# First batch's remainder moved to the third batch, zero tile first, and late halves ahead of the last block's values

## The chip, the cores and the metric

The kernel runs on one core of one Trainium2 chip. The metric is the time on the device in microseconds (us). A core has five engines with their own queues: PE (matmul), DVE (vector), ACT (scalar), POOL (GpSimd) and SP, which here only issues transfers. PE writes to PSUM; DVE and ACT read PSUM; POOL works on SBUF only and also issues transfers.

## The reference, cut to what matters

Batch is 8, heads 8, sequence 576, head size 64; the feed-forward part has 4608 rows of 512 and a hidden size of 1536.

```python
kv = einsum('bhsd,bhse->bhde', k, v)          # per head 64 x 64, no softmax
o  = einsum('bhsd,bhde->bhse', q, kv)
x  = o / sqrt(mean(o*o, -1) + 1e-6) * g_norm  # norm over the head
x  = x.transpose(0, 2, 1, 3).reshape(4608, 512)
xn = x / sqrt(mean(x*x, -1) + 1e-6) * rms_g   # norm over the row
out = (silu(xn @ w_gate) * (xn @ w_val)) @ w_out
```

## The kernel before, in words

**Tiling.** A batch has 576 rows: four chunks of 128 (512 "main" rows) and a remainder of 64. The feed-forward part runs in nine groups of 512 rows: the main rows of each of the eight batches, and one group (number 8, run as the last but one) of the eight remainders, whose x is gathered in the tile `xr`. A group has 24 slots, a gate and a value product for each of 12 blocks of 128 hidden columns (`slots_a`, four matmuls of 512 columns each), and 16 slots of the output product (`slots_b`). Gate goes through silu on ACT (L686), value is multiplied with it on DVE (L695, tile `h`).

**Attention.** For a batch the kernel computes k times v (`kv`), q transposed (`qT`), o, the two sums of squares that both norms need, and from them one factor per row and head (`chain`), then `xna` = o times factor, and x as the transpose of it. In batches 2 to 7 this is placed among the slots of the group before: `place_attention` hands every operation to a planner (`Placer`), which knows a cost and a room per slot and engine and puts an operation in the first slot in which it fits; `P.at` books one at a fixed slot. There the squares are made on ACT (L391, tile `sq`), weighted on POOL (L446), summed on DVE (L454), the product `xna` on DVE (L521, L526), and the transposes are transfers issued by SP (L336 and L338 for q, L583 for x). Batch 1 is placed by hand among the slots of group 0 (`place_second`, its base slot as argument). Inside one slot the operations are issued in the order of booking, PE's behind the slot's own matmuls. All engines take their instructions in that order.

**The lead.** Batch 0 comes first and by hand. PE spins on a tile of zeros, `idle` (`spin`, L238), until k times v can start (`kv_pairs`, L291); chunks 0 and 1 are taken up to x, and then group 0 begins with the first half of its rows (256 columns, L705 and L677) while the weights are still on their way in four blocks (`wg`, `wv`, issued by POOL, L228 and L229). The list `early` holds 22 slots: slot 0 has the first block's three gates, then come its three values, then three gates and three values for each other block. After each slot n, `behind(n)` issues a piece of the attention of chunks 2 and 3 and of the remainder: q's transposes (L310), o transposed (L404), the sums (L429), the chain, o (L371), `xna` (L381) and x's transposes (L552). Then come 12 slots "half" with gate and value of the late 256 rows, and 16 slots "all" of output. POOL casts the remainder of batch 0's q (L216), which SP loads (`load_rem`, L202), and goes on with the loads of batch 1, the output weights (L233) and k and v of batch 2.

**Order of transfers.** A load waits in the queue of the engine that issues it, for what that engine does before it. Some are tied to others by hand: the late half of the first q to the first v, the second broadcast of g to the last gate weights, q of batch 2 to the first output weights.

Of the kernel before, what the change touches and what calls it, by code (L numbers as in the profile page):

```python
# [87 lines left out]
def kernel(  # L88
# [47 lines left out]

    ident = consts.tile([128, 128], BF16, name="ident")
# [22 lines left out]
    for tile_, rows in ((krT, REM // 2), (vr, REM // 2), (rems[0][0], REM)):  # L160
        for r0 in (rows, 2 * rows) if rows < REM else (rows,):
            nc.vector.memset(tile_[r0 : REM if r0 < REM else 128], 0.0)
    idle = consts.tile([128, MAIN], BF16, name="idle")
    nc.vector.memset(idle, 0.0)  # L164
# [78 lines left out]
    class Att:  # L243
        def __init__(self, b):
            self.b = b
            self.kv, self.qT = kvs[b % 2], qTs[b % 2]
            if b < 2:
                self.qTj = self.qT.rearrange("p c j t -> p (c j t)").rearrange("p (j c t) -> p j c t", j=NS, c=NC + 1)
            else:
                self.qTj = self.qT.rearrange("p c j t -> p j c t")  # L250
            self.kv_chunks = range(NC + 1)
            self.o, self.outa, self.sq = {}, {}, {}
            self.xT = {}
            self.st = None
# [79 lines left out]
        def qT_dma(self):  # L334
            flat = mains[self.b, 0].rearrange("p c h d -> p (c h d)")
            nc.sync.dma_start_transpose(out=self.qT[:, 0:NC].rearrange("p c j t -> p (c j) t"), in_=flat)  # L336
            rem = rems[0][self.b % 2][:REM].rearrange("p h d -> p (h d)")
            return nc.sync.dma_start_transpose(out=self.qT[:, NC, :, 0:REM], in_=rem)  # L338

        def o_mm(self, c, pool=None):  # L340
            self.o[c] = o = (pool or att_p).tile([128, H, D], FP32, name={None: "att"}.get(pool, "mm1" if pool is mm1_p else "o2"))
            for j in range(NS):
                nc.tensor.matmul(  # L343
                    o[:, 2 * j : 2 * j + 2, :], lhsT=self.qTj[:, j, c, :], rhs=self.kv[:, j, :, :],
                    start=j == 0, stop=j == NS - 1, skip_group_check=True,
                )
# [14 lines left out]
        def part(self, t, n):  # L361

            if n == NC:
                return t[:, NC]
            return t[:, n // 2 * 2 : n // 2 * 2 + 2, n % 2 : H : 2]
# [11 lines left out]
        def xna_pairs(self, o, js, c0, c1):  # L377
            if not hasattr(self, "xna"):
                self.xna = xna_p.tile([128, NC + 1, H, D], BF16, name="xna")
            h0, h1 = 2 * js[0], 2 * js[-1] + 2  # L380
            nc.vector.tensor_tensor(  # L381
                out=self.xna[:, c0:c1, h0:h1], in0=o,
                in1=self.al[:, c0:c1, h0:h1].to_broadcast([128, c1 - c0, h1 - h0, D]), op=OP.mult,
            )

        def o_of(self, c):
            return self.o[c] if c == NC else self.o["main", c].rearrange("p c h d -> p (c h) d")
# [60 lines left out]
        def red(self, c, which):  # L448
            if self.st is None:
                self.st = stat.tile([128, 2, NC + 1, H], FP32, name="st")  # L450
# [3 lines left out]
            nc.vector.reduce_sum(out=self.part(self.st[:, which], c), in_=of, axis=AX.X)  # L454

        def chain_t(self):
            if not hasattr(self, "al"):
                t = lambda n, dt=FP32, h=H: stat.tile([128, NC + 1, h], dt, name=n)
                self.u, self.r, self.t, self.z, self.nt, self.al = (t(n) for n in ("u", "r", "t", "z", "nt", "al"))
                self.s = stat.tile([128, NC + 1], FP32, name="srow")  # L460
                self.y = t("y", I32)
# [55 lines left out]
        def xna_(self, c, eng, src=None):  # L517
            if not hasattr(self, "xna"):
                self.xna = xna_p.tile([128, NC + 1, H, D], BF16, name="xna")
            if src is None and c < NC:  # L520
                return eng.tensor_tensor(  # L521
                    out=self.part(self.xna, c), in0=self.outa[c].rearrange("p (c h) d -> p c h d", c=2),
                    in1=self.part(self.al, c).to_broadcast([128, 2, H // 2, D]), op=OP.mult,
                )
# [51 lines left out]
        def x_dma(self, c0, c1):  # L576
            if c0 < NC:
                to = self.x_to()[:, c0:c1].rearrange("p c j t -> p (c j) t")
                of = self.xna[:, c0:c1].rearrange("p c h d -> p (c h d)")
            else:  # L580
                to = xr[:, :, self.b * REM : (self.b + 1) * REM]
                of = self.xna[:REM, c0].rearrange("p h d -> p (h d)")
            return nc.sync.dma_start_transpose(out=to, in_=of)  # L583
# [12 lines left out]
    def place_attention(P, b, casts=(), at=0, chain_at=0):  # L596
        a, start = Att(b), at + 2
        V, A = nc.vector, nc.scalar
        N1 = range(NC + 1)
# [7 lines left out]
        for c in N1:  # L607
            p = P.psum(0.24, lambda: a.o_mm(NC), kv + qt) if c == NC else main
            s = P.put("ACT", 0.6, lambda c=c: a.sq_(c), [p])
            outs[c] = P.put("ACT", 0.6, lambda c=c: a.outa_(c), [p])  # L610
            if c >= 2:
                P.tiles[-1 if c == NC else c - 4] += [s, outs[c]]
# [5 lines left out]
        for n in range(0, 13, 4):  # L618
            prev = [P.put("DVE", 0.8, lambda n=n: [f() for f in a.chain(0, NC + 1)[n : n + 4]], prev, chain_at)]
        xn = [P.put("DVE", 0.68, lambda c=c: a.xna_(c, V), prev + [outs[c]]) for c in N1]  # L620
        put = [P.put("SP", 0.0, lambda c=c: a.x_dma(*c), [xn[c[1] - 1]]) for c in ((0, 2), (2, 4), (4, 5))]
# [200 lines left out]
    load_rem(0, 0)  # L822
# [4 lines left out]
    G.memset(rems[0][1][REM:], 0.0)  # L827
# [55 lines left out]
    cast_rem(0, 0, G)  # L883
# [3 lines left out]
    wo_loads = [load_wo(n) for n in range(NF // OB)]  # L887
    for f in loads_kv(2):
        f()
# [8 lines left out]
    steps = {6: (0, 3), 7: (3, 5), 8: (5, 8), 9: (8, 10), 10: (10, 12)}  # L898

    def behind(n):  # L900
# [4 lines left out]
        elif n == 1:  # L905
            a.qT_out(a.qT_mm(ALL, (NC,)), ALL, NC, A)
# [3 lines left out]
        elif n == 4:  # L910
            a.sqT_(a.oT_mm(ALL, NC, NC + 1, o2_p), ALL, NC, NC + 1)
        elif n == 5:
            a.st = None
            a.stat_pairs(P0, 2, 4, att_p, "att")
            a.stat_pairs(P1, 2, 4, att_p, "att")
        elif n == 6:
            a.stat_pairs(ALL, NC, NC + 1, att_p, "att")
        if n in steps:
            for f in a.chain(2, NC + 1)[slice(*steps[n])]:
                f()  # L920
        if n in (8, 9):
            held[n - 8] = a.o_pairs((P0, P1)[n - 8], 2, 4, att_p, "att")
        elif n == 10:
            held[2] = a.o_pairs(ALL, NC, NC + 1, o2_p, "o2")
        if n in (12, 13):
            i = (12, 13).index(n)
# [3 lines left out]
        if n in (15, 16):  # L930
            i = (15, 16).index(n)
# [8 lines left out]
    for n, s in enumerate(early):  # L940
        if n == 12:
            gate = nc.sync.dma_start(out=gbc, in_=g_norm.partition_broadcast(128))
            tc.add_manual_dep(gate.ins, w_loads[-1][0].ins.name, SYNC, reason="the weights come first")
        emit([s])
        behind(n)

    gsq = consts.tile([128, D], FP32, name="gsq")
    G.tensor_tensor(out=gsq, in0=gbc, in1=gbc, op=OP.mult)
    G.tensor_copy(out=g2, in_=gsq.rearrange("p (o d) -> p o d", o=1).to_broadcast([128, H, D]))
    gate = load_q(2)  # L950
    tc.add_manual_dep(gate.ins, wo_loads[0].ins.name, SYNC, reason="the weights come first")
# [11 lines left out]
    for b in range(1, B):  # L963
        if b == 1:
            end = place_second(P, 9)
# [14 lines left out]
        elif b + 1 < B:  # L980
            P.put("SP", 0.0, lambda b=b: load_q(b + 1), at=starts[b - 1] + 6 * (b == 2))
            casts = place_casts(P, b + 1, starts[b - 1] + 18)
            for n, f in enumerate(loads_kv(b + 1)):
                if b == 2:
                    P.at("POOL", 0.85, f, starts[1] + 11 + n)
                else:
                    P.put("POOL", 0.85, f, at=starts[b - 1] + 14)
    emit(slots)
# [28 lines left out]
```

## Time and profile before

| | |
|---|---|
| median of 3 runs | 323.86 us (323.74 to 324.04) |
| profiled execution | 323.98 us |
| its span, first to last instruction | 322.2 us |
| PE busy | 313.7 us |
| DVE busy | 175.4 us |
| ACT busy | 142.9 us |
| POOL busy | 89.0 us |

How to read it: the span leaves out what lies around the instructions, so it is shorter than the time. PE's matmuls overlap and their ends are modelled; for the pace of a run of matmuls the chain of work that ended last is used, which gives pieces with a start, a length and a count. In a timeline the bracket behind an instruction says how long its engine stood idle before it and what ended that. For transfers a row gives the queue, the size and the median time from issue to landing.

### The profile page before, as it was taken

The page shows a single profiled execution, that of the slowest core. Times are in us where ns is not written, and L with a number is a line of the kernel's source. Part 1 is how long each engine was busy: PE and PEld are TensorE (multiplying, and loading weights), DVE is VectorE, ACT ScalarE, POOL GpSimd, SP SyncE. Part 2 cuts the span into 40 slices and gives each one's busy share as a digit, 9 for nine tenths or more (in the row PEclk, how much of TensorE's full clock was granted, in tenths as well). Part 3 has the DMA queues.
Part 4 walks back from the last instruction along what each step waited for, and adds up shares of the span by engine and source line. Part 5 has one row for each costly group of instructions (what it writes and reads, how often), then busy time and mean ns, then how long its engine had stood idle before and what let it go on. Part 6 is the DMA issues. An engine that isn't in the chain of part 4 may idle for free.

```text
span 322.2 us, 5618 instructions
## 1 busy us (share of the span) xinstructions
PE 313.7 (97%) x2158; PEld 160.0 (50%) x2158; DVE 175.4 (54%) x394; ACT 142.9 (44%) x267; POOL 89.0 (28%) x110
## 2 busy tenths in 40 slices
PE   5999999999999999999999999999999999999995
PEld 1678866544444444444444444444444444444443
DVE  4558437487938671768176917781678133203410
ACT  1375466486659322932283227422742233223321
POOL 8763330039006700670058005800420000000000
PEclk9999999999999999999999999999999999999999
DMA  8999999959664994598559956798000600040002
GB/s 213 220 200 199 194 221 220 220 146 144 139 162 130 124 162 141 145 122 144 150 160 102 141 149 181 90 136 167 36 1 0 171 35 0 1 110 22 0 33 100
DMA packets 78358, 40.51 MB, mean 126 GB/s; under 512 B 41976, under 2 KB 73852, under 8 KB 78332
## 3 DMA queue, kind: packets, MB, share of 16 engines
q0 software_dynamic: 30672, 14.16, 34.5%
q1 hardware_dynamic: 46176, 25.01, 31.4%
q10 hardware_dynamic: 1484, 0.99, 1.0%
q8 instruction: 17, 0.28, 0.4%
q14 instruction: 9, 0.07, 0.1%
HBM read 37.78 MB, written 9.44 MB: 147 GB/s over the span
## 4 chain that ended last, share of the span: by engine, by line
PE 97%; DVE 1%; ACT 1%; issue 0%
PE mm L677 58%; PE o L712 27%; PE mm L238 3%; PE att L275 2%; PE mm L712 2%; PE att L343 1%; PE o L356 1%; PE att L552 1%; PE mm L291 0%; PE att L356 0%; PE mm L739 0%; PE o L739 0%; PE mm L705 0%; PE att L321 0%; ACT sqT L415 0%
## 5 line engine op out<-in xcount | busy, mean ns | idle before, releaser
L695 DVE TENSOR_TENSOR h<-silu,mm 128x512 bf16<-128x512 bf16 (+1 forms) x120 | 75.6, 631 | 83.0 <-PE mm L677 73.7
L686 ACT ACTIVATE silu<-mm 128x512 bf16<-128x512 f32 (+1 forms) x120 | 66.4, 557 | 84.2 <-PE mm L677 77.1
L677 PE MATMUL mm<-x,wv 128*128 128x512 bf16 (+1 forms) x432 | 99.9, 356 | 0.0
L677 PE MATMUL mm<-x,wg 128*128 128x512 bf16 (+1 forms) x420 | 98.5, 358 | 0.5 <-DVE h L695 0.5
L712 PE MATMUL o<-wo,h 128*128 128x512 bf16 x396 | 90.1, 379 | 0.0
L446 POOL TENSOR_TENSOR sq<-sq,g 128x512 bf16<-128x512 bf16 x30 | 34.3, 1153 | 130.2 <-ACT sq L391 130.1
L677 PEld LDWEIGHTS <-wv 128*128 128x128 bf16 x480 | 46.2, 98 | 45.2
L677 PEld LDWEIGHTS <-wg 128*128 128x128 bf16 x468 | 45.0, 98 | 45.4 <-issue 1.0
L712 PEld LDWEIGHTS <-h 128*128 128x128 bf16 x420 | 40.2, 98 | 46.0 <-DVE h L695 0.2
L728 ACT COPY osb<-o 128x512 f32<-128x512 f32 x33 | 19.2, 586 | 69.1 <-PE o L712 69.1
L454 DVE TENSOR_REDUCE st<-sq 128x8 f32<-128x512 bf16 x60 | 38.4, 677 | 1.8 <-POOL sq L446 1.7
L304 DVE CAST kvs<-att 64x256 bf16<-64x256 f32 x14 | 5.9, 422 | 30.0 <-PE att L275 29.8
L521 DVE TENSOR_TENSOR xna<-outa,al 128x512 bf16<-128x512 bf16 x24 | 15.0, 684 | 0.0
L238 PE MATMUL mm<-idle 128*128 128x512 bf16 x27 | 8.7, 493 | 4.0 <-DVE idle L164 4.0
L677 PE MATMUL mm<-xr,wg 128*128 128x512 bf16 x48 | 12.3, 379 | 0.0
L677 PE MATMUL mm<-xr,wv 128*128 128x512 bf16 x48 | 12.3, 379 | 0.0
L209 POOL CAST main_q<-stg 128x1024 bf16<-128x1024 f32 (+1 forms) x12 | 11.3, 970 | 0.4 <-DMA stg<-in_q_dram 0.4
L391 ACT ACTIVATE sq<-att 128x512 bf16<-128x512 f32 x18 | 11.1, 618 | 0.0
L395 ACT CAST outa<-att 128x512 bf16<-128x512 f32 x18 | 10.9, 604 | 0.0
L834 ACT ACTIVATE wv<-wv,gain 128x384 bf16<-128x384 bf16 x16 | 9.0, 608 | 0.4 <-PE mm L677 0.4
L195 POOL DMA_DIRECT2D vc<-in_v_dram x9 | 7.8, 864 | 1.8 <-PE mm L677 1.8
L238 PEld LDWEIGHTS <-idle 128*128 128x128 bf16 x31 | 3.6, 119 | 8.6 <-DVE idle L164 4.0
(139 smaller groups left out, 195.3 us busy)
## 6 DMA issues: line engine op xcount, KB each, us to landing
out_dram<-osb SPq DMA_DIRECT2D x31, 256.0 KB, 2.6
stg<-in_q_dram SPq DMA_DIRECT2D x6, 1024.0 KB, 6.8
vc<-in_v_dram POOLq DMA_DIRECT2D x7, 512.0 KB, 8.0
kc<-in_k_dram POOLq DMA_DIRECT2D x7, 512.0 KB, 6.2
wg<-in_moe_w_gate_dram POOLq DMA_DIRECT2D x4, 384.0 KB, 15.8
wv<-in_moe_w_val_dram POOLq DMA_DIRECT2D x4, 384.0 KB, 17.1
wo<-in_moe_w_out_dram POOLq DMA_DIRECT2D x4, 384.0 KB, 13.1
out_dram<-osb SPq DMA_DIRECT2D x9, 128.0 KB, 2.3
```

The costliest lines, as they stand in the source:

```text
L209: return copy(out=mains[b, t][:, cs[0] : cs[1], h0:h1, :], in_=staged[b, t].rearrange("p h (c d) -> p c h d", c=NC)[:, cs[0] : cs[1], h0:h ...
L238: nc.tensor.matmul(ps, lhsT=idle[:, :128], rhs=idle[:, : ps.shape[-1]], start=True, stop=True, skip_group_check=True)
L391: nc.scalar.activation(out=self.sq[c][:, 0], in_=self.o_of(c), func=ACT.Square)
L395: nc.scalar.copy(out=self.outa[c], in_=self.o_of(c))
L446: eng.tensor_tensor(out=self.sq[c][:, 1], in0=self.sq[c][:, 0], in1=g2, op=OP.mult)
L454: nc.vector.reduce_sum(out=self.part(self.st[:, which], c), in_=of, axis=AX.X)
L521: return eng.tensor_tensor(out=self.part(self.xna, c), in0=self.outa[c].rearrange("p (c h) d -> p c h d", c=2), in1=self.part(self.al, c). ...
L677: nc.tensor.matmul(ps[:, : c1 - c0], lhsT=w[n][:, s, jj * 128 : (jj + 1) * 128], rhs=x_of(g, s, c0, c1), start=s == 0, stop=s == NS - 1)
L686: nc.scalar.activation(out=sis[g, j][:, c0:c1], in_=ps, func=ACT.Silu)
L695: nc.vector.tensor_tensor(out=hs[g, j][:, c0:c1], in0=sis[g, j][:, c0:c1], in1=v_ps, op=OP.mult)
L712: nc.tensor.matmul(ps, lhsT=hs[g, j][:, t * 128 : (t + 1) * 128], rhs=wo[j // OB][:, j % OB, :], start=j == 0, stop=j == NF - 1)
L728: (eng.copy if eng is nc.scalar else eng.tensor_copy)(out=o, in_=ps)
```

## The change

- `idle` is declared and zeroed first, ahead of the other memsets on DVE.
- The remainder of batch 0 leaves the lead: its load on SP, its cast on POOL, and its q transposes, o transposed, sums, o, `xna` and x's transposes in `behind`. The chain of the lead covers chunks 2 and 3 only, and what is left in `behind` goes one slot sooner.
- Its q is loaded later by POOL into `q0r`, behind the output weights and ahead of the next k and v; SP turns it into `q0T` between the two transposes of batch 2; batch 2's attention has six chunks in place of five, the sixth with batch 0's q and kv. For that batch 0 gets a kv tile of its own (three `kvs` in place of two), POOL clears `kvs[0]`, `q0T` and the unused columns of `qTs[0]`, and a fourth transpose of x is issued.
- Of the 22 early slots the last three (the values of the last weight block) come behind the first three "half" slots (late rows, first weight block).
- Batch 1 is placed one slot later (base 10 for 9). The four issues of batch 3's k and v keep their slots, but are booked ahead of batch 2's attention, so the planner counts them when it places that, and inside a slot they come first.

```diff
+    idle = consts.tile([128, MAIN], BF16, name="idle")
+    nc.vector.memset(idle, 0.0)
...
-    kvs = [consts.tile([128, NS, 2, D], BF16, name=f"kvs{n}") for n in range(2)]
+    kvs = [consts.tile([128, NS, 2, D], BF16, name=f"kvs{n}") for n in range(3)]
...
+    q0r = consts.tile([REM, H, D], BF16, name="q0r")
+    q0T = consts.tile([128, NS, 128], BF16, name="q0T")
...
-            self.kv, self.qT = kvs[b % 2], qTs[b % 2]
+            self.kv, self.qT = kvs[b % 2 if b else 2], qTs[b % 2]
+            self.chunks = NC + 1 + (b == 2)
...
+            if self.b == 2:
+                nc.sync.dma_start_transpose(out=q0T[:, :, 0:REM], in_=q0r.rearrange("p h d -> p (h d)"))
             return nc.sync.dma_start_transpose(out=self.qT[:, NC, :, 0:REM], in_=rem)
...
+                q_, kv_ = (self.qTj[:, j, c, :], self.kv) if c <= NC else (q0T[:, j, :], kvs[2])
                 nc.tensor.matmul(
-                    o[:, 2 * j : 2 * j + 2, :], lhsT=self.qTj[:, j, c, :], rhs=self.kv[:, j, :, :],
+                    o[:, 2 * j : 2 * j + 2, :], lhsT=q_, rhs=kv_[:, j, :, :],
...
-        N1 = range(NC + 1)
+        N1 = range(a.chunks)
...
-        put = [P.put("SP", 0.0, lambda c=c: a.x_dma(*c), [xn[c[1] - 1]]) for c in ((0, 2), (2, 4), (4, 5))]
+        put = [P.put("SP", 0.0, lambda c=c: a.x_dma(*c), [xn[c[1] - 1]]) for c in ((0, 2), (2, 4), (4, 5), (5, 6))[: a.chunks - 2]]
...
-    load_rem(0, 0)
-    G.memset(rems[0][1][REM:], 0.0)
+    G.memset(kvs[0], 0.0)
...
-    cast_rem(0, 0, G)
...
     wo_loads = [load_wo(n) for n in range(NF // OB)]
+    G.dma_start(out=q0r, in_=q[0, :, MAIN:S, :].rearrange("h p d -> p h d"))
+    G.memset(q0T, 0.0)
     for f in loads_kv(2):
...
-    steps = {6: (0, 3), 7: (3, 5), 8: (5, 8), 9: (8, 10), 10: (10, 12)}
+    steps = {5: (0, 4), 7: (4, 6), 8: (6, 8), 9: (8, 12)}
...
-        elif n == 1:
-            a.qT_out(a.qT_mm(ALL, (NC,)), ALL, NC, A)
-        elif n == 4:
-            a.sqT_(a.oT_mm(ALL, NC, NC + 1, o2_p), ALL, NC, NC + 1)
-        elif n == 6:
-            a.stat_pairs(ALL, NC, NC + 1, att_p, "att")
-        elif n == 10:
-            held[2] = a.o_pairs(ALL, NC, NC + 1, o2_p, "o2")
-        elif n == 15:
-            a.xna_pairs(held[2], ALL, NC, NC + 1)
-        elif n == 18:
-            a.xT_mm(ALL, (NC,))
-            for j in ALL:
-                a.xT_out(j, (NC,), A)
...
+        if b == 2:
+            for n, f in enumerate(loads_kv(b + 1)):
+                P.at("POOL", 0.85, f, starts[1] + 11 + n)
         if b == 1:
-            end = place_second(P, 9)
+            end = place_second(P, 10)
...
-    emit(slots)
+    cut = len(early) - FB[-1]
+    lead(0, cut)
+    emit(slots[: FB[0]])
+    lead(cut, len(early))
+    G.memset(qTs[0][:, NC, :, REM:], 0.0)
+    emit(slots[FB[0] :])
```

More of the change, by code (lines that the diff above doesn't have):

```diff
@@ L159 @@
     xr = consts.tile([128, NS, MAIN], BF16, name="xr")
[L160 to L164, printed above, removed]
+    for tile_ in (krT, vr):
+        for r0, r1 in ((REM // 2, REM), (REM, 128)):
+            nc.vector.memset(tile_[r0:r1], 0.0)
     nc.vector.memset(diag, 0.0)
@@ L378, in xna_pairs @@
             if not hasattr(self, "xna"):
-                self.xna = xna_p.tile([128, NC + 1, H, D], BF16, name="xna")
+                self.xna = xna_p.tile([128, NC + 2, H, D], BF16, name="xna")
             h0, h1 = 2 * js[0], 2 * js[-1] + 2
@@ L518, in xna_ @@
             if not hasattr(self, "xna"):
-                self.xna = xna_p.tile([128, NC + 1, H, D], BF16, name="xna")
+                self.xna = xna_p.tile([128, NC + 2, H, D], BF16, name="xna")
             if src is None and c < NC:
@@ L580, in x_dma @@
             else:
-                to = xr[:, :, self.b * REM : (self.b + 1) * REM]
+                b = self.b if c0 == NC else 0
+                to = xr[:, :, b * REM : (b + 1) * REM]
                 of = self.xna[:REM, c0].rearrange("p h d -> p (h d)")
@@ L618, in place_attention @@
         for n in range(0, 13, 4):
-            prev = [P.put("DVE", 0.8, lambda n=n: [f() for f in a.chain(0, NC + 1)[n : n + 4]], prev, chain_at)]
+            prev = [P.put("DVE", 0.8, lambda n=n: [f() for f in a.chain(0, a.chunks)[n : n + 4]], prev, chain_at)]
         xn = [P.put("DVE", 0.68, lambda c=c: a.xna_(c, V), prev + [outs[c]]) for c in N1]
-        put = [P.put("SP", 0.0, lambda c=c: a.x_dma(*c), [xn[c[1] - 1]]) for c in ((0, 2), (2, 4), (4, 5))]
+        put = [P.put("SP", 0.0, lambda c=c: a.x_dma(*c), [xn[c[1] - 1]]) for c in ((0, 2), (2, 4), (4, 5), (5, 6))[: a.chunks - 2]]
         return put[2 if b == B - 1 else 1][1] + X_SLOTS
@@ L915, in behind @@
             a.stat_pairs(P1, 2, 4, att_p, "att")
[L916 to L917 removed]
         if n in steps:
[L919 removed]
+            for f in a.chain(2, NC)[slice(*steps[n])]:
                 f()
[L921 to L926 removed]
+        if n in (7, 8):
+            held[n - 7] = a.o_pairs((P0, P1)[n - 7], 2, 4, att_p, "att")
+        if n in (11, 12):
+            i = (11, 12).index(n)
             a.xna_pairs(held[i], (P0, P1)[i], 2, 4)
[L928 to L931 removed]
+        elif n in (14, 15):
+            i = (14, 15).index(n)
             a.xT_mm((P0, P1)[i], (2, 3), None if i else o2_p)
@@ L934, in behind, with lead @@
                 a.xT_out(j, (2, 3), A)
-        elif n == 18:
-            a.xT_mm(ALL, (NC,))
-            for j in ALL:
-                a.xT_out(j, (NC,), A)
[L940 to L951, printed above, removed]
+    def lead(n0, n1):
+        for n in range(n0, n1):
+            if n == 12:
+                gate = nc.sync.dma_start(out=gbc, in_=g_norm.partition_broadcast(128))
+                tc.add_manual_dep(gate.ins, w_loads[-1][0].ins.name, SYNC, reason="the weights come first")
+            emit([early[n]])
+            behind(n)
     def one(two):
@@ L982 @@
             casts = place_casts(P, b + 1, starts[b - 1] + 18)
[L983 to L987, printed above, removed]
-    emit(slots)
+            for f in loads_kv(b + 1) if b > 2 else ():
+                P.put("POOL", 0.85, f, at=starts[b - 1] + 14)
+    cut = len(early) - FB[-1]
+    lead(0, cut)
+    emit(slots[: FB[0]])
+    lead(cut, len(early))
+    gsq = consts.tile([128, D], FP32, name="gsq")
+    G.memset(qTs[0][:, NC, :, REM:], 0.0)
+    G.tensor_tensor(out=gsq, in0=gbc, in1=gbc, op=OP.mult)
+    G.tensor_copy(out=g2, in_=gsq.rearrange("p (o d) -> p o d", o=1).to_broadcast([128, H, D]))
+    gate = load_q(2)
+    tc.add_manual_dep(gate.ins, wo_loads[0].ins.name, SYNC, reason="the weights come first")
+    emit(slots[FB[0] :])
 _INS = ['q', 'k', 'v', 'g_norm', 'moe_w_gate', 'moe_w_val', 'moe_w_out', 'moe_rms_g']
```

16 lines of the change are left out of this document (8 added, 8 removed).

## The prediction

> **What bounds the kernel now.** I read the page's busy table first, then the list of who waited for whom, then the chain of work that ended last from its start, and last the timelines of the stretches that the change touches.
>
> The busy table, and the two waits of TensorE that matter here (total us, times, longest):
>
> ```profile
> PE 313.7 (97%) x2158; PEld 160.0 (50%) x2158; DVE 175.4 (54%) x394; ACT 142.9 (44%) x267; POOL 89.0 (28%) x110
> ```
>
> ```profile
> PE mm L238 <- DVE idle L164: 4.0, 1, 4.0
> PE mm L677 <- DVE h L695: 0.5, 1, 0.5
> ```
>
> TensorE is the bound: 8.5 us of the 322.2 us are not matmul, and 4.0 of these are the wait for the zero tile. So a matmul taken away, or a wait ended, is worth its whole length, unless TensorE then waits for something else. The lead (batch 0, up to about 35 us) is where that must be tested. Its chain, start and length in us:
>
> ```profile
> 3.66 0.28 DVE idle L164
> 3.99 7.45 PE mm L238 x22
> 11.44 0.67 PE mm L291 x12
> ...
> 12.71 0.78 PE mm L291 x12
> ...
> 20.75 0.22 PE att L310 x4
> ...
> 22.72 0.22 PE o L404 x4
> ...
> 24.01 0.08 PE att L429 x4
> ...
> 26.31 0.22 PE o L371 x4
> 26.53 2.20 PE mm L677 x20
> ...
> 28.95 0.44 PE mm L677 x4
> ...
> 30.59 0.19 PE att L552 x4
> 30.78 6.65 PE mm L677 x60
> ```
>
> The reader sees TensorE in an unbroken chain from 3.99 us, at 6.65 / 60 = 0.111 us for a 256-column matmul: 1.33 us for three half slots of one kind (12 matmuls), 2.66 us for three gate and value pairs (24). L291 is the first batch's k times v; the five groups of four with 0.22, 0.22, 0.08, 0.22 and 0.19 us are the remainder chunk of batch 0. At 28.95 us the gates of the last weight block begin, at 30.78 us its values, and after them (30.78 + 1.33 + 2.66) the first three late halves end at 34.77 us.
>
> **The change part by part.** *1. Zero tile first.* The vector engine's first memset starts at 0.91 us; the zero tile takes its place, so the spin can start at about 1.24 instead of 3.99 us (0.91 + 0.28, and the 0.05 us seen now). What the spin leads to, k times v, needs these (DVE, then POOL issues, then landings of the v loads counted from the issue):
>
> ```profile
> 0.91 1.11 DVE L162 MEMSET remk<- 32x512 uint32 x2 [0.91 <-PEq L1001]
> ...
> 10.06 0.69 DVE L209 CAST main_q<-stg 128x1024 bf16<-128x1024 f32 x1 [1.17 <-DMA stg<-in_q_dram]
> ```
>
> ```profile
> 2.08 1.52 POOL L195 DMA_DIRECT2D vc<-in_v_dram  x2
> ```
>
> ```profile
> vc<-in_v_dram POOLq DMA_DIRECT2D x1, 256.0 KB, 8.2
> ```
>
> ```profile
> vc<-in_v_dram POOLq DMA_DIRECT2D x2, 256.0 KB, 8.5
> ```
>
> The first half of v lands at 2.08 + 8.2 = 10.28 us. The second is issued at 2.84 us; a median of 8.5 us with one at 8.2 makes the other 8.8, so 11.64 us. Spin of the present length ends at 1.24 + 7.45 = 8.69 us, so the first twelve matmuls start at 10.3 us instead of 11.44, the q transposes behind them have their cast by 10.75, and the second twelve start at 11.64 instead of 12.71: the start gains 1.07 us, not the 2.75 us by which the spin moves; v takes the rest. From below: at the slow spacing throughout (22 at 0.44 us, twice 0.22) the spin ends at 10.9 and the second twelve start at about 12.2 us, gain 0.5 us. From above nothing more than 1.07 comes, v being the limit.
>
> *2. Remainder of batch 0 out of the lead.* Five groups go: 0.22 + 0.22 + 0.08 + 0.22 + 0.19 = 0.93 us of TensorE, 0.74 of it ahead of 28.95 us. Their ACT and DVE operations go too; these were beside TensorE and I count nothing for them. From here the weights limit:
>
> ```profile
> 8.90 0.74 POOL L229 DMA_DIRECT2D wv<-in_moe_w_val_dram  x1 [0.66 <-DMA remv<-in_v_dram]
> ...
> 10.56 0.74 POOL L228 DMA_DIRECT2D wg<-in_moe_w_gate_dram  x1 [0.92 <-DMA vc<-in_v_dram]
> ```
>
> ```profile
> 9.04 0.75 SPq L202 DMA_DIRECT2D rstg<-in_q_dram  x1
> ```
>
> ```profile
> wv<-in_moe_w_val_dram POOLq DMA_DIRECT2D x1, 384.0 KB, 17.9
> ...
> rstg<-in_q_dram SPq DMA_DIRECT2D x1, 128.0 KB, 10.4
> ```
>
> ```profile
> wg<-in_moe_w_gate_dram POOLq DMA_DIRECT2D x1, 384.0 KB, 18.1
> ```
>
> ```profile
> 10.00:28.70 18.70, 17.97 (x198) 14.50 (x197) 12.11 (x44) 9.71 (x22) 11.37 (x18) 1.00 1.30 209
> ```
>
> The third block's values land at 26.8 us, the fourth's gates at 28.66, that is 0.29 us ahead of their use at 28.95: the cover is nearly gone already. The transfers run full through the whole stretch (last two numbers: share 1.30, 209 GB/s). The remainder load of 128 KB (issued 9.04, landed 19.44) leaves this stretch: 131072 B at 209 GB/s is 0.63 us, by which later weights come sooner. Below, the weights gain nothing, if what goes is not what they share; above, any gain of 0.9 us or more makes TensorE the limit again. I take 0.63, from the nearest row. In the Trainium skill, "DMA: Bandwidth & Descriptors", section "Specifications", pieces under 512 B are said to miss line rate; a remainder row of one head is 64 floats, 256 B. By that rule the load would cost more than its bytes, the sum would go towards the upper end, and no row here times one such load alone.
>
> TensorE alone would reach the third block's values at 26.53 + 8 x 0.111 - 1.07 - 0.74 = 25.61 us; they land at 26.8 - 0.63 = 26.17. Three value slots (1.33) and the two transposes of chunks 2 and 3 (0.45) follow, to 27.95. The last gates land at 28.03.
>
> *3. Late halves of the first block ahead of the last values.* From 28.03: gates 1.33, late halves 2.66, values 1.33, end 33.35 us against 34.77, a gain of 1.42. The move has no cost of its own: the same 24 + 12 matmuls. The values are reached at 32.02 us, after the 30.78 at which they were there before; in the old order they would have been asked for at 29.36. With the weights no earlier (28.66): 33.98, gain 0.79. With TensorE alone the limit: 1.07 + 0.93 = 2.00.
>
> *4. Queues.* On SP the 0.75 us issue at 9.04 goes, with nothing behind it for long. On POOL the cast of the remainder (and its wait) goes; a remainder load, a memset of its tile and one of the old queries' columns come behind the output weights, and ahead of the next k and v. On SP a third transpose stands between the two of batch 2, with stores and the next q load behind it:
>
> ```profile
> 58.50 1.18 SPq L338 DMA_TRANSPOSE qTs<-remq  x1
> ```
>
> ```profile
> 66.64 0.41 PE L356 MATMUL o<-kvs,qTs 64*128 64x64 bf16 x16
> ```
>
> The last transpose is issued 1.2 us later, about 59.7 us, 7 us ahead of its use; I count nothing. Batch 1 is planned one slot later (0.9 us) and still ends at the slot in which its x is first wanted; nothing too, and at worst the 0.9 us.
>
> *5. The chunk in batch 2.* TensorE: four matmuls as now for chunk 4, 0.22 us, no cover. POOL one weighted square, DVE two sums and one product, ACT two operations, in the first full group:
>
> ```profile
> 69.11 0.22 PE att L343 x4
> ```
>
> ```profile
> L446 POOL TENSOR_TENSOR sq<-sq,g 128x512 bf16<-128x512 bf16 x30 | 34.3, 1153 | 130.2 <-ACT sq L391 130.1
> L454 DVE TENSOR_REDUCE st<-sq 128x8 f32<-128x512 bf16 x60 | 38.4, 677 | 1.8 <-POOL sq L446 1.7
> L521 DVE TENSOR_TENSOR xna<-outa,al 128x512 bf16<-128x512 bf16 x24 | 15.0, 684 | 0.0
> ```
>
> ```profile
> 58.90:93.20 34.30, 33.77 (x261) 15.88 (x259) 24.13 (x56) 21.18 (x40) 11.42 (x12) 1.00 0.82 165
> ```
>
> DVE gets 2 x 0.677 + 0.684 = 2.04 us more beside 24.13 of 34.3, POOL 1.15 beside 11.42. That fits, so nothing if spread. But there is a stall in this group:
>
> ```profile
> 71.59 0.94 POOL L195 DMA_DIRECT2D kc<-in_k_dram  x1
> ```
>
> ```profile
> 77.17 0.69 DVE L454 TENSOR_REDUCE st<-sq 128x8 f32<-128x512 bf16 x1 [0.85 <-POOL sq L446]
> ```
>
> ```profile
> 78.50 1.02 PE L677 MATMUL mm<-x,wg 128*128 128x512 bf16 x4 [0.53 <-DVE h L695]
> ```
>
> The issues of the next k and v stand between the weighted squares on POOL; a sum on DVE waits for its square, an h product waits behind the sum, and TensorE waits 0.53 us for the h. In the change the planner books these four issues before it places the squares, so the later squares and sums go to later slots. Gone, that is -0.53; with one more square and two more sums it may as well come back (0), or grow by up to what is added. I take half, -0.27.
>
> The x of the next group must still come in time:
>
> ```profile
> 86.31 2.61 SPq L583 DMA_TRANSPOSE x<-xna  x2
> ```
>
> ```profile
> x<-xna SPq DMA_TRANSPOSE x12, 3.3
> ```
>
> ```profile
> 93.23 1.03 PE L677 MATMUL mm<-x,wg 128*128 128x512 bf16 x4
> ```
>
> The second transpose is issued near 87.6 and lands near 90.9, 2.3 us early; TensorE comes 1.2 to 1.5 us sooner and DVE has 1.4 us more ahead of it, which is about that cover: no cost, and up to 0.6 us.
>
> *Sum:* -1.42 + 0.22 - 0.27 = -1.47 us. The profiled execution took 323.98 us (span 322.2), 0.12 above the median of 323.86. So 322.51 for such an execution, 322.4 us against the median.
>
> **The rivals.** *Weights no earlier.* The lead gains 0.79: -0.79 + 0.22 - 0.27 = -0.84, 323.0 us. For it: other engines' loads keep the transfers full. Against: they share one rate, and it is the load ahead that leaves.
>
> *The vector engine crowds (slower).* If the added DVE work stands ahead of the h products in group 1, as the sum at 77.17 does, its 2.04 us come onto TensorE: -1.42 + 0.22 + 2.04 = +0.84, 324.7 us; with the POOL square's 1.15 also, 325.9. It decides from 1.85 us of new stall on (0.65 is the edge of "same"). For it: the stall exists. Against: DVE is 70% busy there, and the longer sequence has the slots of the output stage to go to.
>
> *The clock falls back in the new pause.* The spin takes 7.45 us for 22 matmuls that at 0.22 us are 4.84: 2.61 us go to a slow beginning. Now a pause of 1.6 us (8.69 to 10.3; up to 4.2 if the whole spin were fast) comes behind it. If the slow beginning were paid again, the start would lose 1.54 instead of gaining 1.07; nothing waits for weights then, and the lead ends at 34.77 + 1.54 - 0.93 = 35.38: +0.61 + 0.22 - 0.27 = +0.56, 324.4 us, or 324.7 with the old stall. Against: the 0.5 us pauses of this trace leave the pace as it was; none is as long as 1.6. The Trainium skill, "TensorE: Matmul & The Clock Gate", section "What's actually happening", gives one idle window of about 3.4 us before the clock halves; by it the 1.6 us pause costs nothing.
>
> *The change only moves the wait.* If wg3's landing slipped because more loads are issued earlier on POOL (it no longer waits for the remainder), the lead would gain about 0.3: 323.5 us. Against: those loads stand behind the weights.
>
> **How the numbers follow.** What the runs can tell from no change is about 0.2%, 0.65 us: 323.2 to 324.5 is "same". Forecast (lead gains 1.1 to 2.0, stall between gone and as it was) 0.62, 321.5 to 323.2; weights no earlier 0.08, at 323.0; wait only moved 0.06, at 323.5; crowding 0.14, 324.0 to 325.9; clock 0.10, 324.4 to 324.7. Faster: 0.62 + 0.04 of the second. Same: the other 0.04 of the second, the 0.06 of the third and 0.05 of the last two, 0.15. Slower: the 0.19 that is left of the last two. The range runs from all gains at once (-2.00 + 0.22 - 0.53 = -2.31, 321.55) to the crowding's price, 324.7.
>
> **What would show it.** The zero tile's memset at 0.9 and the spin at 1.2 us; a pause ahead of L291 until about 10.3, released by vc; the last gates starting near 28.0, waiting for wg; turn of q for batch 1 some 0.5 us sooner than 37.43 (one slot more lies ahead of it); the first full group's gate near 57.5, 1.4 us sooner than now; the wait for h near 78 gone or changed. Wrong would be a spin as slow at its end as at its start, L291 later than 11, wg landing at 28.7 or later, or waits for h of over 1 us in group 1.

## The result, and the profile after

The changed kernel takes 322.0 us (median of 6, 321.78 to 323.17) against 323.96 (median of 6, 323.74 to 324.04): ratio 0.9948, 95% interval 0.9932 to 0.9963. The profiled execution took 321.78 us (span 320.0) against 323.98 (322.2), so 2.2 us less; the forecast was 1.5 us less.

Line numbers in the changed kernel are 2 to 7 higher: the spin is L240, k times v in the lead L294, gate and value L684, the product of hidden and output L719, the weighted square L452, the sum on DVE L460.

The busy table of the page after, and what TensorE waited for (total us, times, longest):

```profile
PE 313.0 (98%) x2142; PEld 159.3 (50%) x2142; DVE 176.3 (55%) x395; ACT 142.3 (44%) x263; POOL 90.8 (28%) x113
```

```profile
PE mm L294 <- DMA vc<-in_v_dram: 1.7, 1, 1.7
PE mm L240 <- DVE idle L138: 1.2, 1, 1.2
PE o L558 <- DVE xna L387: 0.5, 1, 0.5
PE mm L684 <- DMA wv<-in_moe_w_val_dram: 0.2, 1, 0.2
```

The 4.0 us wait for the zero tile is now 1.2, a wait of 1.7 us for v has come behind the spin, a small one for a weight block stands in the lead, and the wait for `h` in group 1 is gone from the list. TensorE's timeline after (start, length, what; in the bracket the idle time before it):

```profile
1.19 7.47 PE L240 MATMUL mm<-idle 128*128 128x512 bf16 x22 [1.19 <-DVE idle L138]
10.32 0.38 PE L294 MATMUL mm<-vc,main_k 128*128 128x128 bf16 x4 [1.66 <-DMA vc<-in_v_dram]
...
11.68 0.40 PE L294 MATMUL mm<-vc,main_k 128*128 128x128 bf16 x4
...
25.89 1.05 PE L684 MATMUL mm<-x,wv 128*128 128x256 bf16 x8 [0.23 <-DMA wv<-in_moe_w_val_dram]
...
27.81 1.92 PE L684 MATMUL mm<-x,wg 128*128 128x256 bf16 x16
```

The last weight block's gates begin at 27.81 us (28.03 forecast) and run on without a gap into the late halves (x16 is three gates and the first late gate). The landings behind these two starts, POOL's issue and the time from issue to landing, for the third block's values and the fourth's gates:

```profile
8.79 0.74 POOL L231 DMA_DIRECT2D wv<-in_moe_w_val_dram  x1 [0.56 <-DMA remv<-in_v_dram]
10.56 0.74 POOL L230 DMA_DIRECT2D wg<-in_moe_w_gate_dram  x1 [1.03 <-DMA vc<-in_v_dram]
```

```profile
wv<-in_moe_w_val_dram POOLq DMA_DIRECT2D x1, 384.0 KB, 17.1
```

```profile
wg<-in_moe_w_gate_dram POOLq DMA_DIRECT2D x1, 384.0 KB, 17.2
```

By these rows they land at 25.89 and 27.76 us (issue plus time to landing), 0.9 us sooner than the 26.8 and 28.66 of before, and TensorE starts on each within 0.1 us of its landing. In group 1:

```profile
57.20 1.03 PE L684 MATMUL mm<-x,wg 128*128 128x512 bf16 x4
...
91.12 1.03 PE L684 MATMUL mm<-x,wg 128*128 128x512 bf16 x4
```

```profile
72.33 4.54 POOL L452 TENSOR_TENSOR sq<-sq,g 128x512 bf16<-128x512 bf16 x4
```

The same gate in the timeline before:

```profile
58.78 0.59 PE L677 MATMUL mm<-x,wg 128*128 128x512 bf16 x2
```

Group 1's first gate starts at 57.20 against 58.78, so the lead has gained 1.58 us. Group 2's first gate starts at 91.12 against 93.23: group 1 takes 0.53 us less, though it holds 0.22 us more matmul. The four issues of the next k and v no longer split the last weighted squares, which run as one block of four.

### The profile page after: what moved, and what is told of

Same layout as the page of the kernel before. It is cut to its first block, busy times and chain, and to the rows that moved or that the text cites. A ratio compares the mean times of both kernels' runs of the same rounds, so it can differ in the third digit from the quotient of the medians.

```text
span 320.0 us, 5586 instructions
## 1 busy us (share of the span) xinstructions
PE 313.0 (98%) x2142; PEld 159.3 (50%) x2142; DVE 176.3 (55%) x395; ACT 142.3 (44%) x263; POOL 90.8 (28%) x113
## 4 chain that ended last, share of the span: by engine, by line
PE 91%; DMA 8%; issue 0%; DVE 0%; ACT 0%; POOLq 0%
PE mm L684 57%; PE o L719 27%; DMA wv<-in_moe_w_val_dram 5%; DMA remv<-in_v_dram 2%; PE att L278 2%; PE mm L719 2%; PE att L349 1%; PE o L362 1%; PE att L362 0%; PE mm L746 0%; PE o L746 0%; PE att L324 0%; PE att L558 0%; PE att L410 0%; PE att L445 0%
## 5 line engine op out<-in xcount | busy, mean ns | idle before, releaser
L684 PE MATMUL mm<-x,wv 128*128 128x512 bf16 (+1 forms) x432 | 99.9, 356 | 0.2 <-DMA wv<-in_moe_w_val_dram 0.2
L684 PE MATMUL mm<-x,wg 128*128 128x512 bf16 (+1 forms) x420 | 97.9, 358 | 0.0
L719 PE MATMUL o<-wo,h 128*128 128x512 bf16 x396 | 90.0, 379 | 0.0
L452 POOL TENSOR_TENSOR sq<-sq,g 128x512 bf16<-128x512 bf16 x31 | 35.4, 1151 | 126.5 <-ACT sq L397 126.5
L684 PEld LDWEIGHTS <-wv 128*128 128x128 bf16 x480 | 46.2, 98 | 45.4 <-DMA wv<-in_moe_w_val_dram 0.5
L684 PEld LDWEIGHTS <-wg 128*128 128x128 bf16 x468 | 45.1, 98 | 44.9 <-DMA wg<-in_moe_w_gate_dram 0.2
L719 PEld LDWEIGHTS <-h 128*128 128x128 bf16 x420 | 40.2, 98 | 45.8
L460 DVE TENSOR_REDUCE st<-sq 128x8 f32<-128x512 bf16 x62 | 39.7, 677 | 0.2
L684 PE MATMUL mm<-xr,wv 128*128 128x512 bf16 x48 | 12.3, 379 | 0.0
L684 PE MATMUL mm<-xr,wg 128*128 128x512 bf16 x48 | 12.3, 379 | 0.0
L240 PE MATMUL mm<-idle 128*128 128x512 bf16 x27 | 8.7, 492 | 1.2 <-DVE idle L138 1.2
L719 PE MATMUL mm<-wo,h 128*128 128x512 bf16 x24 | 7.8, 379 | 0.0
```

The lines of the kernel that those rows point to most:

```text
L452: eng.tensor_tensor(out=self.sq[c][:, 1], in0=self.sq[c][:, 0], in1=g2, op=OP.mult)
L684: nc.tensor.matmul(ps[:, : c1 - c0], lhsT=w[n][:, s, jj * 128 : (jj + 1) * 128], rhs=x_of(g, s, c0, c1), start=s == 0, stop=s == NS - 1)
L719: nc.tensor.matmul(ps, lhsT=hs[g, j][:, t * 128 : (t + 1) * 128], rhs=wo[j // OB][:, j % OB, :], start=j == 0, stop=j == NF - 1)
```

## The experiments

The time at which TensorE turns batch 1's q (L324, in the chain) marks the end of the lead: 36.72 us in the changed kernel. Five traces in this document have that same lead, with the spin of 18 or of 25, and turn q at 36.67, 36.72, 36.80, 36.90 and 36.91 us; so a difference of 0.2 us between two single traces says nothing.

### The changed kernel again

> The changed kernel once more, beside the three that follow. Theory (the new pause of 1.7 us between spin and k times v is mostly harmless, but in some executions the clock falls back in it): most executions at 321.8 us with a granted clock of 1.000, and about one in three 0.8 to 1.4 us longer with a clock of 0.995. Rival (the two long executions of the first measurement were something else): none with a lower clock, spread as in the kernel before, 0.3 us.

Five executions: 321.72, 321.61, 322.66, 322.23 and 321.69 us; ratio 0.9939 (0.9925 to 0.9953). With the first six there are eleven, of which three (322.60, 322.66, 323.17 us) have a granted clock of 0.995, the other eight 1.000. That is about one in four and not one in three, at the cost expected.

### The zero tile behind the other memsets again

```diff
-    idle = consts.tile([128, MAIN], BF16, name="idle")       # ahead of all
-    nc.vector.memset(idle, 0.0)
...
+    idle = consts.tile([128, MAIN], BF16, name="idle")       # ahead of diag, as before
+    nc.vector.memset(idle, 0.0)
```

> The zero tile goes back behind the other memsets, everything else stays. Theory (TensorE's early start counts, up to what the weights give): the first k times v matmul at 11.3 instead of 10.3 us, no pause ahead of it; the third block's values are reached at about 26.6, after they have landed at 25.9, so 0.7 us is lost to the end of the lead: 322.5 us, and all executions alike, since there is no pause in which the clock could fall. Rival (the lead is bound by the weights alone, the start is worth nothing): 321.9 us.

322.23 us (321.85 to 322.38); 0.9942 (0.9929 to 0.9956). TensorE's timeline:

```profile
3.71 7.67 PE L240 MATMUL mm<-idle 128*128 128x512 bf16 x22 [3.71 <-DVE idle L166]
11.21 0.39 PE L294 MATMUL mm<-vc,main_k 128*128 128x128 bf16 x4
...
26.40 1.04 PE L684 MATMUL mm<-x,wv 128*128 128x256 bf16 x8
```

k times v starts 0.89 us later, the third block's values 0.51 us later and without a wait; batch 1's q is turned at 37.32, 0.60 us later, and the time is 0.5 us longer than that of the runs above. So of the 0.9 us that the early tile gives at the start 0.5 to 0.6 reaches the end, and the wait for the weights takes the rest. No execution here went below a clock of 0.998.

### The zero tile first, and nothing else

```diff
 # the kernel before
+    idle = consts.tile([128, MAIN], BF16, name="idle")       # ahead of all memsets
+    nc.vector.memset(idle, 0.0)
```

> The kernel before with nothing changed but the zero tile first. Theory (the weights bind the old lead): the start gains 1.0 us, but the last gates land at 28.66 and the last values at 30.66 as before, against a use at 28.95 and 30.78, so all but 0.1 us of it is lost again: 323.8 us, with waits for wg and wv of together some 0.9 us. Rival (the start is worth its whole length): 322.9 us.

324.05 us beside 324.05; 1.0003 (0.9994 to 1.0011). TensorE's timeline and its chain:

```profile
10.38 0.38 PE L291 MATMUL mm<-vc,main_k 128*128 128x128 bf16 x4 [1.43 <-DMA vc<-in_v_dram]
...
20.25 0.40 PE L310 MATMUL att<-ident,remq 128*128 128x128 bf16 x4 [0.41 <-POOL remq L216]
...
26.81 0.60 PE L677 MATMUL mm<-x,wg 128*128 128x256 bf16 x4 [0.16 <-DVE h L695]
27.24 1.47 PE L677 MATMUL mm<-x,wv 128*128 128x256 bf16 x12
...
28.77 0.60 PE L677 MATMUL mm<-x,wg 128*128 128x256 bf16 x4
...
30.74 0.50 PE L677 MATMUL mm<-x,wv 128*128 128x256 bf16 x3
```

```profile
9.23 10.31 DMA rstg<-in_q_dram
...
19.59 0.62 POOL remq L216
...
20.25 0.40 PE att L310 x4
...
26.34 0.42 DVE h L695
...
26.81 1.91 PE mm L677 x16
...
37.46 1.24 PE att L321 x40
```

It starts 0.9 us sooner and is back on the old times at the third block's values, at 27.24 us (27.26 before); the last block's gates and values come at 28.77 and 30.74 (28.79 and 30.67 in the same view of before), q's turn at 37.46 (37.43). The time is what the theory said, but the reason is another: no wait for a weight stands in this trace. The chain runs through the remainder of batch 0. Its load lands, POOL casts it, and only then can TensorE turn it, at 20.25 us (20.58 before), so 0.6 of the 0.9 us are gone there. The rest goes at 26.81 us, where TensorE waits for an `h` on DVE. The weights would have allowed hardly more: by issue and time to landing the last gates come at 28.72 us, 0.05 us ahead of their use. So the old lead had two limits close together, and the change moves both, since the remainder's work leaves the lead together with its load. In the old kernel the early start was worth nothing, in the new one 0.5 us: the parts of the change are not worth a fixed sum each.

### The early slots in one piece

```diff
-    cut = len(early) - FB[-1]
+    cut = len(early)
```

> The early slots in one piece, the three late halves of the first block behind them as before. Theory: the last block's values are then asked for at 27.83 + 1.33 = 29.2 us and land at about 29.7, so TensorE waits some 0.5 us for wv: 322.3 us. Rival (they are there in time, the reorder does nothing): 321.8 us and no wait for wv at 29 us.

322.69 us (322.41 to 322.84); 0.996 (0.9948 to 0.9973). The loss is 0.7 to 1.0 us, more than the theory or its rival said, and no wait for wv shows, because the profiled execution is one of the three in which the clock fell. TensorE's timeline, and two stretches of the same execution (the columns behind the lengths are PE, PEld, DVE, ACT, POOL, then the granted clock, the share of the transfers and GB/s):

```profile
1.19 6.45 PE L240 MATMUL mm<-idle 128*128 128x512 bf16 x22 [1.19 <-DVE idle L138]
10.03 0.38 PE L294 MATMUL mm<-vc,main_k 128*128 128x128 bf16 x4 [2.39 <-DMA vc<-in_v_dram]
...
11.46 0.61 PE L294 MATMUL mm<-vc,main_k 128*128 128x128 bf16 x4
```

```profile
10.09:13.50 3.41, 3.41 (x37) 3.07 (x37) 2.12 (x10) 0.88 (x3) 2.57 (x5) 0.66 1.32 213
13.50:16.91 3.41, 3.40 (x29) 1.85 (x26) 1.49 (x6) 1.70 (x5) 2.34 (x6) 0.84 1.25 233
```

The spin ended early (6.45 us long), the pause was 2.4 us, the first four matmuls took 0.38 us and four of the same shape, 1.4 us later, 0.61. A mean clock of 0.66 and 0.84 is half pace for 0.34 x 3.41 / 0.5 + 0.16 x 3.41 / 0.5 = 3.4 us. The order and the clock are mixed here, so the next run has the longer spin.

### The early slots in one piece, with a longer spin

```diff
-    cut = len(early) - FB[-1]
+    cut = len(early)
...
-    spin(mm1_p.tile([128, MAIN], FP32, name="mm1"), 18)
+    spin(mm1_p.tile([128, MAIN], FP32, name="mm1"), 25)
```

> The early slots in one piece again, with the spin of 25 that leaves no pause. Theory (the old order asks for the last values before they land): a wait for wv of 0.5 to 0.7 us near 29.5 us in the profile, 322.4 us, no long executions. Rival (the 0.7 to 1.0 us that the old order lost came from the clock falling in the pause): 321.8 us.

322.41 us (322.37 to 322.58); 0.995 (0.9938 to 0.9962). The timelines of TensorE's matmuls and of its weight loads (PEld), POOL's issue of the last values and their time to landing:

```profile
1.19 7.82 PE L240 MATMUL mm<-idle 128*128 128x512 bf16 x29 [1.19 <-DVE idle L138]
10.18 0.38 PE L294 MATMUL mm<-vc,main_k 128*128 128x128 bf16 x4 [1.17 <-DMA vc<-in_v_dram]
...
29.71 1.49 PE L684 MATMUL mm<-x,wv 128*128 128x256 bf16 x12 [0.43 <-ACT silu L693]
```

```profile
29.71 1.21 PEld L684 LDWEIGHTS <-wv 128*128 128x128 bf16 x12 [0.71 <-DMA wv<-in_moe_w_val_dram]
```

```profile
11.75 0.74 POOL L231 DMA_DIRECT2D wv<-in_moe_w_val_dram  x1 [0.59 <-DMA vc<-in_v_dram]
```

```profile
wv<-in_moe_w_val_dram POOLq DMA_DIRECT2D x1, 384.0 KB, 17.9
```

The values land at 29.65 us and their matmuls start at 29.71, after 0.43 us idle. The matmul's bracket names a silu; the bracket of the weight load ahead of it names wv, and the landing agrees with that. A wait for several things is put down to the one that came last, so both rows are needed. The time is 0.55 us longer than the 321.86 us of the same spin in the new order; the theory holds. The longer spin did not fill the pause here: its matmuls (four more than the number given, as in every run here) took 7.82 us, and 1.17 us of pause were left, but the clock stayed at 1.000. (In the execution of the run above with the fallen clock TensorE was late enough to need no such wait; there the two losses hide each other.)

### The remainder load in its old place

```diff
+    load_rem(0, 0)          # on SP, behind the late half of the first q; nothing reads it
```

> The 128 KB remainder load is issued again in its old place on SP, though nothing reads it; all else as in the changed kernel. Theory (this load stood in the way of the weights): the last gates land near 28.6 instead of 27.8 us, the lead ends 0.6 to 0.9 us later, 322.4 to 322.7 us. Rival (the weights came sooner for another reason, or TensorE is the limit): wg lands as now, 321.8 us.

323.12 us (322.86 to 323.84); 0.9975 (0.9965 to 0.9984): 1.4 us lost, twice what was expected. Two things could be mixed in, the clock and the size of the pieces in which the load is moved, so two more runs, both with the spin of 25, differ in the load alone.

```diff
+    load_rem(0, 0)          # 128 KB in 512 pieces of 256 B
```

> The remainder load back on SP (64 rows of 8 pieces of 256 B, 128 KB), with the spin of 25; nothing reads it. Theory (it delays the weights by more than its bytes): the last gates land 0.9 to 1.3 us later than without it and the time is 322.9 to 323.1 us. Rival (part of the 1.4 us lost with the short spin came from the clock): 322.4 us, which is its bytes at 209 GB/s.

323.13 us (322.71 to 323.48); 0.9973 (0.9961 to 0.9984).

```diff
+    scratch = rstage.tile([REM, H, D], FP32, name="rstg")
+    nc.sync.dma_start(      # 128 KB in 64 pieces of 2 KB
+        out=scratch.rearrange("p h d -> p (h d)"), in_=q[0, 0, 0:MAIN, :].rearrange("(p c) d -> p (c d)", c=MAIN // REM)
+    )
```

> In its place a load of the same 128 KB in 64 pieces of 2 KB, other rows of q, read by nothing; spin of 25. Theory (bytes alone do not make the cost, the small pieces do): half or less of what the load in 256 B pieces costs, 322.2 to 322.5 us. Rival (bytes decide): the same time as with 256 B pieces.

322.63 us (322.48 to 322.69); 0.9955 (0.9942 to 0.9967). The issue and the landing of the last gates, and the turn of q: first with 256 B, then with 2 KB.

```profile
10.61 0.74 POOL L230 DMA_DIRECT2D wg<-in_moe_w_gate_dram  x1 [0.85 <-DMA vc<-in_v_dram]
```

```profile
wg<-in_moe_w_gate_dram POOLq DMA_DIRECT2D x1, 384.0 KB, 18.4
```

```profile
37.96 1.24 PE att L324 x40
```

```profile
10.52 0.74 POOL L230 DMA_DIRECT2D wg<-in_moe_w_gate_dram  x1 [0.93 <-DMA vc<-in_v_dram]
```

```profile
wg<-in_moe_w_gate_dram POOLq DMA_DIRECT2D x1, 384.0 KB, 17.4
```

```profile
36.91 1.24 PE att L324 x40
```

Without the load (the spin of 25 again, below) the gates land at 10.54 + 17.3 = 27.84 and q is turned at 36.80. So 128 KB in 256 B pieces push the weights back by 1.2 us and the lead by 1.16; the same bytes in 2 KB pieces by 0.1 and 0.11, which is no more than single traces of one kernel differ by. The pieces decide. The time with 2 KB is nevertheless 0.8 us longer than without. Of this the profiled executions show 0.5: the last store is issued 0.11 us later (317.66 for 317.55), and the span ends 2.9 us behind it and not 2.55. That end is 0.4 us longer in all three kernels with the unread load and in no other; why stays open. So 0.4 us of the losses of these three belong to the probe and not to the change.

### The four issues booked late again

```diff
-        if b == 2:
-            for n, f in enumerate(loads_kv(b + 1)):
-                P.at("POOL", 0.85, f, starts[1] + 11 + n)
...
+            for n, f in enumerate(loads_kv(b + 1)):      # behind batch 2's attention, same slots
+                if b == 2:
+                    P.at("POOL", 0.85, f, starts[1] + 11 + n)
```

> The four issues of batch 3's k and v are booked after batch 2's attention again, in the same slots; all else as in the changed kernel. Theory (the planner's not knowing them made the wait for h near 78 us): the wait comes back at 0.5 to 0.9 us, and with six chunks perhaps more: 322.4 to 322.8 us. Rival (the wait went because group 1 starts sooner or the slots shifted): 321.8 us.

322.99 us (322.40 to 323.65); 0.9969 (0.9956 to 0.9981). Three of the six executions are at a clock of 0.995 and above 323.3, the other three at 322.40 to 322.58, 0.7 us above the changed kernel's like ones. DVE's and TensorE's timeline:

```profile
75.78 0.69 DVE L460 TENSOR_REDUCE st<-sq 128x8 f32<-128x512 bf16 x1 [0.85 <-POOL sq L452]
```

```profile
77.11 1.02 PE L684 MATMUL mm<-x,wg 128*128 128x512 bf16 x3 [0.31 <-DVE h L702]
```

The sum on DVE waits 0.85 us for its square again, as it did before the change, and TensorE for the `h` behind it. From k times v of batch 2 to that of batch 3 (L278 in the chain) it is 90.49 - 61.87 = 28.62 us here, and 89.78 - 61.68 = 28.10 in the changed kernel: 0.52 us from the order of booking alone.

### A longer spin, and a shorter one

```diff
-    spin(mm1_p.tile([128, MAIN], FP32, name="mm1"), 18)
+    spin(mm1_p.tile([128, MAIN], FP32, name="mm1"), 25)
```

> The spin gets seven matmuls more (25 for 18), which at 0.22 us fill 1.5 of the 1.7 us pause. Theory (the pause is where the clock falls in some executions): the same best time, 321.8 us, and no execution with a clock under 1.000; where the slow beginning is longer, the spin may end late by a few tenths. Rival (clock and pause have nothing to do with each other): long executions as often as in the changed kernel.

321.84 us (321.58 to 321.96); 0.9932 (0.992 to 0.9944).

> The changed kernel with the spin of 25 once more, beside the three others. Theory: 321.8 us, all executions within 0.4 us, none with a clock under 0.998. Rival (the five even executions of the first time were chance): one in three 0.8 to 1.4 us longer at 0.995.

321.86 us (321.56 to 322.19); 0.9933 (0.9919 to 0.9946). Ten executions: mean 321.83 us, none above 322.19, none below a clock of 0.999. The changed kernel's eleven: mean 322.12, up to 323.17. The best time is the same; what the filler buys is that no execution loses the 0.8 to 1.4 us. It is the best version found.

```diff
-    spin(mm1_p.tile([128, MAIN], FP32, name="mm1"), 18)
+    spin(mm1_p.tile([128, MAIN], FP32, name="mm1"), 8)
```

> The spin gets ten matmuls fewer (8 for 18), so the pause ahead of k times v grows from 1.7 to about 4 us. Theory (a pause lets the clock fall back, more surely the longer it is): the matmuls behind the pause run at half pace for some us in most executions, the granted clock is below 1.000, and the time is 1 to 2.7 us longer, 322.8 to 324.5 us. Rival (only the warm-up ahead counts, the pause is harmless): 321.8 us in most executions.

324.15 us (322.97 to 324.40), as slow as the kernel before: 0.9994 (0.9984 to 1.0004). All twelve executions show a granted clock of 0.989 to 0.994. TensorE's timeline and two stretches of the profiled one:

```profile
10.28 0.58 PE L294 MATMUL mm<-vc,main_k 128*128 128x128 bf16 x4 [4.08 <-DMA vc<-in_v_dram]
```

```profile
8.43:11.84 3.41, 1.56 (x16) 1.56 (x16) 1.37 (x3) 1.04 (x1) 1.49 (x2) 0.61 1.39 202
11.84:15.26 3.42, 3.42 (x27) 2.81 (x26) 2.28 (x9) 1.18 (x2) 3.35 (x7) 0.50 1.23 235
```

After a pause of 4.1 us the first matmuls already run at half pace (0.58 us for 0.38), and TensorE stays there to the end of the second stretch, at 15.26 us. Here it is the filler work alone that was taken away, and the whole gain of the change is gone.

## Why the prediction was right

The direction, the range and nearly all steps held; sizes were off.

*Zero tile first.* Expected: k times v at 10.3 and its second half at 11.64, limited by v. Measured 10.32 and 11.68, and the wait at the first is put down to v. That v limits the second half is not shown: it follows 1.36 us behind the first with no idle time before it, just as before the change (11.28 and 12.64). In these rows the start gains 0.96 us and not 1.07, because the forecast compared a landing with a start of the chain (11.44), which counts later than the timeline does (11.28). The 0.29 us of cover at 28.95 are too large for the same reason: the timeline has these gates at 28.79.

*Weights as the limit.* Expected starts 26.17 and 28.03 us, measured 25.89 and 27.81. The lead gained 1.58 us and not 1.42, because the term for the remainder load was mis-sized: 0.63 us from its bytes at 209 GB/s, while the weights came 0.9 us sooner, and the probe gives 1.16 us for this load and 0.11 for the same bytes in 2 KB pieces. The rate of the stretch was the wrong row to price it by. That a gain of 0.9 us makes TensorE the limit again does not follow from the prediction's own figures, by which it takes 26.8 - 25.61 = 1.19 us; measured, the weights came 0.9 us sooner and TensorE still waited 0.2 us for them. The Trainium skill's sentence in "DMA: Bandwidth & Descriptors", section "Specifications", that pieces under 512 B miss line rate, had the right sign, and these runs agree with it (1.16 us for 256 B, 0.11 for 2 KB).

*Late halves ahead of the last values.* Expected: in the old order the values would have been asked for at 29.36 us, ahead of their landing. Undone, this costs 0.55 us, with the wait at 29.71.

*Chunk in batch 2.* Four matmuls, 0.22 us, no other trace of it: DVE has 26.0 of 33.8 us busy in group 1 and TensorE does not wait there. The stall was booked at half, -0.27; it went whole, and it was larger than its bracket. Group 1 is 0.53 us shorter with 0.22 us more work, so 0.75 us of stall are gone: before, the gate of the stall starts 1.55 us behind the slot ahead of it (76.95 and 78.50) where slots follow at 0.86, which is 0.69 us, and the bracket said 0.53 because the ends of matmuls are modelled. The order of booking alone gives 0.52 of the 0.75; what gives the rest was not measured apart.

*Sum.* -1.58 in the lead and -0.53 in group 1 are -2.11 of the -2.2 us between the profiled executions, against -1.47. Both terms that were off, the load and the stall, were taken too small, so the forecast was not right by errors that cancel. Medians show -1.96, partly because two of the six executions lost time to the clock; the four at 1.000 have a median of 321.9 us.

*The rivals.* The fall of the clock had a chance of 0.10 and a price of 2.61 us in every execution. It comes in three executions of eleven and costs 0.8 to 1.4 us. The step that failed is the one that took the spin's length for fixed, the pause for 1.6 us each time, and the rival for all or nothing. The same 22 matmuls took 6.45 us in the one trace where the clock fell after them, with a pause of 2.4 us, and 7.45 to 7.75 us in the others. The crowding of the vector engine did not happen, and the weights did land earlier. That the remainder's load, cast and transposes held the old lead up as soon as TensorE came sooner was not in the prediction, which counted nothing for work beside TensorE; its sum did not need it, because that work left the lead in the same change.

## What to carry to other kernels

Where limits lie close together, here TensorE, the landing of weights about 0.1 us ahead of their use, and the remainder's load and cast, price the parts of a change together: the early start was worth 0 us alone and 0.5 with the rest. Take a load of small pieces out of the stretch in which a large one is awaited, and look at the piece size before the bytes. When an expectation's time comes true, still follow the chain: with the zero tile alone the time was as expected and the reason was not. Book what has a fixed place before you let a planner fill in the rest, and when a warm-up moves forward, lengthen it so that it reaches the first real work.

## What the runs showed of the hardware

A pause of 2.4 us was enough for the clock of TensorE to fall to half. Five kernels have the zero tile first and the spin of 18 (the changed kernel, run twice, and four variants of it or of the old one). Their six traces show pauses between spin and first work of 1.27, 1.43, 1.50, 1.66, 1.76 and 2.39 us, and the clock fell only behind the last. Of their 42 executions 15 have a granted clock of 0.994 or 0.995; the pause is known only where there is a trace, so whether one of 1.3 to 1.8 us can be enough is open. With a pause of 4.1 us in the trace (the spin of 8) the clock was 0.994 or less in 12 of 12. The kernels with the late zero tile, and the 26 executions with the spin of 25, whose traces show pauses of up to 1.2 us, had none below 0.998.

The fallen clock stayed at half for 3.4 us in the trace with 2.4 us of pause, and after the pause of 4.1 us for (0.39 x 3.41 + 0.50 x 3.42 + 0.11 x 3.41) / 0.5 = 6.8 us, with the next stretch of that trace:

```profile
15.26:18.67 3.41, 2.86 (x25) 1.63 (x25) 2.31 (x8) 1.73 (x4) 2.81 (x6) 0.89 1.30 212
```

The Trainium skill, "TensorE: Matmul & The Clock Gate", section "What's actually happening", says that the clock is judged in windows of about 3.4 us that run on by themselves, and falls after an idle one. The length of the half-pace stretches, one and two such windows, agrees. That a whole window must be idle does not: 2.4 us were enough in the trace shown. That a window only partly busy counts as idle would fit. By an estimate from the two stretches of that trace the half pace begins at 13.50 - 0.34 x 3.41 / 0.5 = 11.18 us, and the 3.41 us before it hold the whole pause and the 1.15 us of work behind it. It would also fit that the place of the pause in the window makes the fall chance; neither was measured apart.
